# Conditioning vector, input and modulation in one layout: two small loads instead of five

## The chip, the cores and the metric

The kernel runs on one core of a Trainium2 chip. The metric is device time in microseconds (us), the median over several executions. Times inside the profile come from one profiled execution of the kernel and are measured from the start of its span. The engines are TensorE (PE in the profile, its weight loads PEld), VectorE (DVE), ScalarE (ACT), GpSimd (POOL) and SyncE (SP), which issues all loads here.

## The reference

One decode step of a transformer block whose layer norms are modulated by a conditioning vector (adaLN). Two batch elements with one token each, model width 512, 32 query heads of 128 on 8 key/value heads, a cache of 32768 positions of which the last 4096 are used, a feed-forward width of 1792. All data are float32.

```python
mod = (silu(c) @ w_mod).reshape(2, 6, 1, 512)
sa, ca, ga, sb, cb, gb = (mod[:, i] for i in range(6))
h = layernorm(x) * (1 + ca) + sa
q = (h @ wq)                                  # 32 heads of 128
p = softmax(q @ k_cache[:, :, -4096:].T / sqrt(128))
o = p @ v_cache[:, :, -4096:]                 # each of 8 kv heads serves 4 query heads
x = x + ga * (o @ wo)
h = layernorm(x) * (1 + cb) + sb
out = x + gb * (silu(h @ w1) @ w2)
```

The shapes: c and x (2, 512), w_mod (512, 3072), wq (512, 4096), wo (4096, 512), w1 (512, 1792), w2 (1792, 512), and 2 MB of keys and 2 MB of values for each of the 16 pairs of batch element and kv head.

## The kernel before

**The stream.** All large loads go through one ring of eight buffers of 16 KB per partition (`stream`, L69), and all of them are issued on the SyncE queue in the order of the program: four row blocks of w_mod (`wm`), four of wq (`wqt`), then per kv head two loads of keys and two of values (`load_k`, `load_v`), then wo in four loads, w1 in three and w2 in five (`load_runs`, L91). A load waits until the buffer that it takes has been read for the last time by the engine that uses it, eight loads before. `load_rows` (L72) reads 128 successive rows of a weight, one row per partition. `load_runs` gives partition p the rows lo to hi of the group of rows that starts at p times `per`, so that a partition's piece is contiguous in memory and the pieces of neighbouring partitions stand `per` rows apart.

**Two layouts of a vector of 512.** Both put the two batch elements' 512 numbers on eight partitions that lie 16 apart (`rows8`, L104), since VectorE transposes blocks of 32 x 32. In the spread form partition 32g + 16b holds the 128 successive numbers of group g; `turned` (L268) transposes it with a stride of 4 elements, after which partition p holds the numbers 4p to 4p + 3. In the other form, here called the chunk form (names ending in `_ch`), the row holds four runs of 32 numbers that stand 128 apart; a plain transpose (L235 for `cT`, L263 for `hq_T`) then gives partition p the numbers p, 128 + p, 256 + p and 384 + p. The layout of a transposed vector must agree with the rows of the weight that it multiplies: chunk form with 128 successive rows, spread form with rows 4p + k.

**The start.** c and x are loaded in the chunk form, by one load for each batch element (L107), between the first and the second load of w_mod. VectorE transposes c, ScalarE and VectorE form silu (`silu_exp`), and TensorE multiplies with w_mod: shift and scale of the first norm go to `m_ch` (L246) in the chunk form, the other four modulation vectors to `m_sp` (L249) in the spread form. Layer-norm statistics of x come from `moments` (L209). The modulated `h_a` is transposed to `hq_T` and multiplied with wq (L285), and the queries are laid out for the attention. x is read a second time in the spread form (`x_sp`, L474), in the program between the loads of wo and w1, for the residual additions (`xT` at L475, L613).

**The middle.** For each kv head, VectorE transposes the keys (`keys`, L337), TensorE forms scores (L349), then follow the maxima, exponentials, their transposition and the product with the values (L423). `inorder` fixes the order of the instructions of this part on their engines; outside it the framework chooses the order from data dependencies.

**The end.** wo, the second norm, w1, silu and w2 are worked off as their loads land; small matmuls on unused data (`busy`, L534) lie between them. One store of 4 KB (L656) writes the output.

Of the kernel before, what the change touches and what calls it, by code (L numbers as in the profile page):

```python
# [10 lines left out]
ALU = mybir.AluOpType  # L11
AX = mybir.AxisListType

P = 128
B, D = 2, 512
HQ, HKV, DH = 32, 8, 128
# [7 lines left out]
def adaln_block(  # L24
# [16 lines left out]

    nc = tc.nc
    SK = k_cache.shape[2]
    W = min(4096, max(256, SK // 4))
# [14 lines left out]
    def const(shape, name):  # L63
        return consts.tile(shape, F32, name=name)

    def bank(tag, name):
        return (psum1 if tag in "CO" else psum).tile([P, 512], F32, tag=tag, name=name)

    def stream(name):  # L69
        return ring.tile([P, 4096], F32, tag="st", name=name)  # L70

    def load_rows(name, w, k, width):  # L72
        t = stream(f"{name}{k}")[:, :width]
        nc.sync.dma_start(t, w[k * P : (k + 1) * P, :])
        return t

    def load_k(b, h):
        t = stream(f"k{h}_{b}")
        nc.sync.dma_start(
            t, k_cache[b, h, SK - W :, :].rearrange("(p n) d -> p (n d)", p=P)  # L80
        )
        return t
# [8 lines left out]
    def load_runs(name, w, per, lo, hi):  # L91

        e = w.shape[1]
        t = stream(f"{name}{lo}")[:, : (hi - lo) * e].rearrange("p (q e) -> p q e", e=e)
        nc.sync.dma_start(t, w.rearrange("(p q) e -> p q e", q=per)[:, lo:hi, :])
        return t


    x2 = x.rearrange("b s d -> (b s) d")
    x_sp, x_ch, c_ch = const([P, P], "x_sp"), const([P, P], "x_ch"), const([P, P], "c_ch")  # L100
    for t in (c_ch, x_ch, x_sp):
        nc.vector.memset(t, 0.0)
    wm = [load_rows("wm", w_mod, 0, 6 * D)]
    rows8 = lambda t: t.rearrange("(ab r) m -> ab r m", r=16)[:, 0, :]  # L104
    for t, src in ((c_ch, c), (x_ch, x2)):
        for b in range(B):
            nc.sync.dma_start(  # L107
                rows8(t)[b : 2 * 4 : 2, :].rearrange("a (k c) -> a k c", k=4),
                src[b, :].rearrange("(k a c) -> a k c", k=4, a=4),
            )  # L110
# [82 lines left out]

    oTn = const([P, 32, 32], "oTn")
    nc.gpsimd.memset(oTn, 0.0)
    mod_ch = const([P, 2, P], "mod_ch")
# [36 lines left out]

    cT = const([P, 4, 32], "cT")
    nc.vector.transpose(cT.rearrange("p k r -> p (k r)"), c_ch)  # L235
    sg = silu_exp(cT, "sgc", [P, 4, 32])
    scT = const([P, 4, 32], "scT")
    nc.vector.tensor_mul(scT, cT, sg)
    m_ch = bank("A", "m_ch")[:, : 2 * P]
    m_sp = bank("D", "m_sp")  # L240
    for k in range(4):
        ab = wm[k][:, : 2 * D].rearrange("p (s k a c) -> p a s k c", s=2, k=4, a=4)
        cd = wm[k][:, 2 * D :].rearrange("p (s g m) -> p g s m", s=4, g=4)
        for g in range(4):
            r = slice(32 * g, 32 * g + 32)
            nc.tensor.matmul(m_ch[r, :], scT[:, k, :], ab[:, g], start=(k == 0), stop=(k == 3))  # L246
        for g in range(4):
            r = slice(32 * g, 32 * g + 32)
            nc.tensor.matmul(m_sp[r, :], scT[:, k, :], cd[:, g], start=(k == 0), stop=(k == 3))  # L249
        if k == 0:  # L250
            mean_a, rstd_a = moments(x_ch, "a")
            xn = once.tile([P, P], F32, tag="xp", name="xn_a")
            nc.vector.tensor_scalar(
                xn, x_ch, mean_a, rstd_a, op0=ALU.subtract, op1=ALU.mult
            )

    nc.vector.tensor_copy(mod_ch[:, 0, :], m_ch[:, :P])
    nc.vector.tensor_scalar(mod_ch[:, 1, :], m_ch[:, P:], 1.0, None, op0=ALU.add)
    h_a = once.tile([P, P], F32, tag="pr", name="h_a")
    nc.vector.tensor_mul(h_a, xn, mod_ch[:, 1, :])  # L260
    nc.vector.tensor_add(h_a, h_a, mod_ch[:, 0, :])
    hq_T = const([P, 4, 32], "hq_T")
    nc.vector.transpose(hq_T.rearrange("p k r -> p (k r)"), h_a)  # L263
# [4 lines left out]
    def turned(t, name):  # L268
        o = const([P, 4, 32], name)
        nc.vector.transpose(o, t.rearrange("p (m k) -> p k m", k=4))  # L270
        return o


    hT, uT = const([P, 4, 32], "hT_b"), const([P, F // P, 32], "uT")
# [6 lines left out]
    for k in range(4):  # L281
        wv = wqt[k].rearrange("p (n s g m) -> p n g s m", n=2, s=4, g=G)
        for n in range(2):
            for g in range(G):
# [4 lines left out]
                    start=(k == 0),  # L289
                    stop=(k == 3),  # L290
                )
    for n in range(2):
        qT = once.tile([P, D], F32, tag="wide", name=f"qT{n}").rearrange("p (s j r) -> p s j r", s=4, r=32)
        nc.vector.transpose(qT.rearrange("p s j r -> p (s j r)"), q_ps[n])  # L294
        for g in range(G):
            r = slice(32 * g, 32 * g + 32)
# [8 lines left out]
        for i in range(4):  # L305
            r = slice(32 * i, 32 * i + 32)
# [167 lines left out]
    nc.sync.dma_start(rows8(x_sp), x2.rearrange("b (g m) -> g b m", m=P))  # L474
    xT = turned(x_sp, "xT")  # L475
    w1t = []
    for lo, hi in ((0, 2), (2, 3), (3, 4)):
# [17 lines left out]
    for r in (0, 64):  # L495
# [4 lines left out]
            start=True,  # L500
            stop=True,
# [46 lines left out]
    for q in range(24):  # L548
        g = q % 4
# [4 lines left out]
            start=(q < 4),  # L554
            stop=(q >= 20),
# [3 lines left out]
    for q in range(24, 32):  # L559
        for g in range(4):  # L560
# [4 lines left out]
                start=(q == 24),  # L565
                stop=(q == 31),
# [26 lines left out]
    for k in range(4):  # L593
        for g in range(4):
# [4 lines left out]
                start=(k == 0),  # L599
                stop=(k == 3),  # L600
# [16 lines left out]
    for b in range(B):  # L617
# [5 lines left out]
            op0=ALU.mult,  # L623
            op1=ALU.add,
# [4 lines left out]
    for tt in range(WIDE):  # L629
        g = tt % 4  # L630
# [4 lines left out]
            start=(tt < 4),  # L635
            stop=(tt >= WIDE - 4),
# [4 lines left out]
    for tt in range(WIDE, T2):  # L641
        for g in range(4):
# [4 lines left out]
                start=(tt == WIDE),  # L647
                stop=(tt == T2 - 1),
# [35 lines left out]
```

## Time and profile before

| | |
|---|---|
| median of 3 runs | 237.28 us (236.99 to 237.31) |
| the profiled execution, time | 236.89 us |
| the profiled execution, span | 235.0 us |
| busy: PE, DVE, ACT, POOL | 62%, 49%, 11%, 4% of the span |
| data queue of the DMA engines | 7592 packets, 97.54 MB, 97.5% of the time of 16 engines |
| mean granted clock of TensorE | 0.869 |

The span runs from the first to the last instruction; the rest of the execution's time lies around it. A busy share is an average over all stages. The page also cuts the span into 40 slices of 5.9 us with the busy tenths of each engine and the rate of the DMA traffic, and follows the chain of work that ended last from the end to the start.

### The profile page before, as it was taken

The page shows a single profiled execution, that of the slowest core. Times are in us where ns is not written, and L with a number is a line of the kernel's source. Part 1 is how long each engine was busy: PE and PEld are TensorE (multiplying, and loading weights), DVE is VectorE, ACT ScalarE, POOL GpSimd, SP SyncE. Part 2 cuts the span into 40 slices and gives each one's busy share as a digit, 9 for nine tenths or more (in the row PEclk, how much of TensorE's full clock was granted, in tenths as well). Part 3 has the DMA queues.
Part 4 walks back from the last instruction along what each step waited for, and adds up shares of the span by engine and source line. Part 5 has one row for each costly group of instructions (what it writes and reads, how often), then busy time and mean ns, then how long its engine had stood idle before and what let it go on. Part 6 is the DMA issues. An engine that isn't in the chain of part 4 may idle for free.

```text
span 235.0 us, 2644 instructions
## 1 busy us (share of the span) xinstructions
PE 146.5 (62%) x1094; PEld 45.9 (20%) x1094; DVE 114.6 (49%) x176; ACT 25.4 (11%) x56; POOL 10.3 (4%) x30
## 2 busy tenths in 40 slices
PE   0086546367187577667549519626743967788993
PEld 0032101101011121121112102111211222335332
DVE  0634000793694792693892792595298050002130
ACT  2200000100300200200200200200020021003210
POOL 8600000100000000000000000000000000000000
PEclk9999975759869997999976967965985799999999
DMA  6999999999999999999999999999999999999991
GB/s 253 426 438 427 427 438 427 424 439 427 429 441 424 427 438 427 429 438 424 429 435 429 427 432 432 432 429 432 428 429 429 429 432 429 432 426 422 421 412 56
DMA packets 7603, 97.69 MB, mean 416 GB/s; under 512 B 920, under 2 KB 936, under 8 KB 1576
## 3 DMA queue, kind: packets, MB, share of 16 engines
q1 hardware_dynamic: 7592, 97.54, 97.5%
q8 instruction: 8, 0.13, 0.2%
q14 instruction: 3, 0.02, 0.0%
HBM read 97.53 MB, written 0.00 MB: 415 GB/s over the span
## 4 chain that ended last, share of the span: by engine, by line
DMA 64%; DVE 22%; PE 10%; ACT 2%; issue 1%; SPq 1%; DVEq 0%
DVE kT L337 16%; DMA wo<-in_A_wo_dram 14%; DMA k<-in_A_k_cache_dram 14%; DMA v<-in_A_v_cache_dram 13%; DMA wq<-in_A_wq_dram 13%; DMA w<-in_B_w_dram 7%; PE s L349 5%; DMA wm<-in_w_mod_dram 3%; DVE zp L395 2%; PE o L423 2%; PE q L285 1%; DVE xp L393 1%; ACT pr L381 1%; DVE mx L359 1%; ACT L381 1%
## 5 line engine op out<-in xcount | busy, mean ns | idle before, releaser
L337 DVE STREAM_TRANSPOSE kT<-k 128x1024 f32<-128x1024 f32 x64 | 73.7, 1210 | 1.6 <-DMA k<-in_A_k_cache_dram 1.6
L349 PE MATMUL s<-kT,qbd 128*32 128x512 f32 x256 | 44.5, 670 | 11.2 <-DVE kT L337 11.1
L423 PE MATMUL o<-v,ptb 128*32 128x512 f32 x256 | 38.5, 730 | 19.8 <-DMA v<-in_A_v_cache_dram 19.3
L359 DVE TENSOR_REDUCE mx<-s 128x1 f32<-128x512 f32 x8 | 5.5, 691 | 40.1 <-PE s L349 40.1
L349 PEld LDWEIGHTS s<-kT,qbd 128*32 128x32 f32 x256 | 11.1, 126 | 45.8 <-issue 24.1
L285 PE MATMUL q<-wq,hq_T 128*32 128x512 f32 x64 | 11.2, 836 | 10.1 <-DMA wq<-in_A_wq_dram 10.1
L423 PEld LDWEIGHTS o<-v,ptb 128*32 128x32 f32 x256 | 8.1, 124 | 35.8 <-issue 33.1
L402 PE MATMUL pT<-zp,id 128*32 128x256 f32 x64 | 5.6, 418 | 13.9 <-DVE zp L395 13.9
L379 ACT COPY bias<-bp 128x1 f32<-128x1 f32 x8 | 1.3, 159 | 111.9 <-PE bp L377 111.9
L537 PE MATMUL junk<-selh,id 128*32 128x256 f32 x46 | 11.3, 380 | 0.0
L294 DVE STREAM_TRANSPOSE qT<-q 128x512 f32<-128x512 f32 x2 | 1.4, 718 | 18.6 <-PE q L285 18.3
L395 DVE TENSOR_TENSOR zp<-xp,group 128x1024 f32<-128x1024 f32 x8 | 9.8, 1225 | 0.2
L393 DVE STREAM_TRANSPOSE xp<-pr 128x512 f32<-128x512 f32 x8 | 5.6, 701 | 4.4 <-ACT pr L381 4.4
L217 PE MATMUL mean_a<-mv_a,avg 128*128 128x1 f32 x2 | 0.6, 362 | 10.6 <-DVE mv_a L214 10.6
L361 PE MATMUL mT<-ident,mx 128*1 128x128 f32 x16 | 3.0, 270 | 6.4 <-DVE mx L359 6.4
L550 PE MATMUL acc_o<-wo,oTn 128*32 128x512 f32 x48 | 5.8, 598 | 1.9 <-DMA wo<-in_A_wo_dram 1.6
L537 PEld LDWEIGHTS junk<-selh,id 128*32 128x32 f32 x46 | 5.0, 110 | 6.7 <-issue 3.5
L438 PE MATMUL o_all<-ob,selh 128*64 128x128 f32 x64 | 5.7, 304 | 0.8 <-ACT ob L432 0.8
L270 DVE STREAM_TRANSPOSE xT<-x_sp 128x128 f32<-128x128 f32 x1 | 0.4, 403 | 11.8 <-DMA x_sp<-in_A_x_dram 11.8
L432 ACT COPY ob<-o 128x512 f32<-128x512 f32 x8 | 4.7, 585 | 10.3 <-PE o L423 10.3
L285 PEld LDWEIGHTS q<-wq,hq_T 128*32 128x32 f32 x64 | 2.1, 128 | 18.8 <-DMA wq<-in_A_wq_dram 12.5
L249 PE MATMUL m_sp<-wm,scT 128*32 128x512 f32 x32 | 5.7, 796 | 0.0
(132 smaller groups left out, 95.0 us busy)
## 6 DMA issues: line engine op xcount, KB each, us to landing
k<-in_A_k_cache_dram SPq DMA_DIRECT2D x16, 2048.0 KB, 30.2
v<-in_A_v_cache_dram SPq DMA_DIRECT2D x16, 2048.0 KB, 31.5
wq<-in_A_wq_dram SPq DMA_DIRECT2D x4, 2048.0 KB
wo<-in_A_wo_dram SPq DMA_DIRECT2D x4, 2048.0 KB, 32.3
wm<-in_w_mod_dram SPq DMA_DIRECT2D x4, 1536.0 KB, 10.2
w<-in_B_w_dram SPq DMA_DIRECT2D x2, 1024.0 KB, 23.2
w<-in_B_w_dram SPq DMA_DIRECT2D x1, 1792.0 KB
w<-in_B_w_dram SPq DMA_DIRECT2D x2, 896.0 KB
```

The source lines that it names most:

```text
L249: nc.tensor.matmul(m_sp[r, :], scT[:, k, :], cd[:, g], start=(k == 0), stop=(k == 3))
L285: nc.tensor.matmul(q_ps[n][32 * g : 32 * g + 32, :], hq_T[:, k, :], wv[:, n, g], start=(k == 0), stop=(k == 3),)
L337: inorder(nc.vector.transpose(kT[h, b][:, :, 8 * n4 : 8 * n4 + 8, :].rearrange("p j n k -> p n j k"), kt[h, b][:, n4 * 1024 : (n4 + 1) * 1 ...
L349: inorder(nc.tensor.matmul(s_ps[h][r : r + 32, :], qbd[h // 4][:, h % 4, b, j, :], kT[h, b][:, j, 16 * c : 16 * c + 16, :], start=(j == 0) ...
L359: inorder(nc.vector.tensor_reduce(mx, s_ps[h], axis=AX.X, op=ALU.max))
L393: inorder(nc.vector.transpose(xp, pr[h]))
L395: inorder(nc.vector.tensor_mul(zp, xp[:, None, :, 0:16].to_broadcast([P, 4, 16, 16]), group[:, :, None, None].to_broadcast([P, 4, 16, 16]),))
L402: inorder(nc.tensor.matmul(tp[32 * i : 32 * i + 32, :], id4, zp.rearrange("p a s x -> p (a s) x")[:, :, 4 * i : 4 * i + 4], start=True, st ...
L423: inorder(nc.tensor.matmul(o_ps[h][32 * c : 32 * c + 32, :], ptb[h % 2][:, 256 * b + 32 * w : 256 * b + 32 * w + 32], vt[h, b][:, 512 * w ...
L438: inorder(nc.tensor.matmul(o_all[r : r + 64, :], selh[:, m, HQ - G - G * h : 3 * HQ - G - G * h], o_sb[h][:, m * DH : (m + 1) * DH], start ...
L537: inorder(nc.tensor.matmul(junk[0:32, :256], id4, selh.rearrange("p m y -> p (m y)")[:, :256], start=True, stop=True,))
L550: inorder(nc.tensor.matmul(acc[32 * g : 32 * g + 32, :], oTn[:, q, :], wot[q // 8][:, q % 8, :], start=(q < 4), stop=(q >= 20),))
```

## The change

The chunk form goes. c and x are loaded once each, both batch elements by one load, into the spread form (`c_sp`, `x_sp`) at the place where the four small loads stood; the later load of `x_sp` goes too. Row blocks of w_mod and wq are read by `load_runs` with the rows 4p + k for block k, through the helper `row4`; `load_rows` goes. `cT` and `hq_T` are made by `turned`, which moves ahead of its first use. Shift and scale of the first norm come out in the spread form (`m_a`, `mod_a`), so that the matmuls read runs of 128 columns of w_mod instead of 32. The sizes and numbers of the large loads and of the matmuls stay, and one memset on VectorE goes.

```diff
-    def load_rows(name, w, k, width):
-        t = stream(f"{name}{k}")[:, :width]
-        nc.sync.dma_start(t, w[k * P : (k + 1) * P, :])
-        return t
...
-    x_sp, x_ch, c_ch = const([P, P], "x_sp"), const([P, P], "x_ch"), const([P, P], "c_ch")
-    for t in (c_ch, x_ch, x_sp):
+    x_sp, c_sp = const([P, P], "x_sp"), const([P, P], "c_sp")
+    for t in (c_sp, x_sp):
         nc.vector.memset(t, 0.0)
-    wm = [load_rows("wm", w_mod, 0, 6 * D)]
+    row4 = lambda name, w, k: load_runs(name, w, 4, k, k + 1)[:, 0, :]
+    wm = [row4("wm", w_mod, 0)]
     rows8 = lambda t: t.rearrange("(ab r) m -> ab r m", r=16)[:, 0, :]
-    for t, src in ((c_ch, c), (x_ch, x2)):
-        for b in range(B):
-            nc.sync.dma_start(
-                rows8(t)[b : 2 * 4 : 2, :].rearrange("a (k c) -> a k c", k=4),
-                src[b, :].rearrange("(k a c) -> a k c", k=4, a=4),
-            )
-    wm += [load_rows("wm", w_mod, k, 6 * D) for k in range(1, 4)]
-    wqt = [load_rows("wq", wq, k, HQ * DH) for k in range(4)]
+    for t, src in ((c_sp, c), (x_sp, x2)):
+        nc.sync.dma_start(rows8(t), src.rearrange("b (g m) -> g b m", m=P))
+    wm += [row4("wm", w_mod, k) for k in range(1, 4)]
+    wqt = [row4("wq", wq, k) for k in range(4)]
...
-    cT = const([P, 4, 32], "cT")
-    nc.vector.transpose(cT.rearrange("p k r -> p (k r)"), c_ch)
+    def turned(t, name):
+        o = const([P, 4, 32], name)
+        nc.vector.transpose(o, t.rearrange("p (m k) -> p k m", k=4))
+        return o
+
+    cT = turned(c_sp, "cT")
...
-    m_ch = bank("A", "m_ch")[:, : 2 * P]
+    m_a = bank("A", "m_a")[:, : 2 * P]
...
-        ab = wm[k][:, : 2 * D].rearrange("p (s k a c) -> p a s k c", s=2, k=4, a=4)
+        ab = wm[k][:, : 2 * D].rearrange("p (s g m) -> p g s m", s=2, g=4)
...
-            nc.tensor.matmul(m_ch[r, :], scT[:, k, :], ab[:, g], start=(k == 0), stop=(k == 3))
+            nc.tensor.matmul(m_a[r, :], scT[:, k, :], ab[:, g], start=(k == 0), stop=(k == 3))
...
-            mean_a, rstd_a = moments(x_ch, "a")
+            mean_a, rstd_a = moments(x_sp, "a")
...
-    hq_T = const([P, 4, 32], "hq_T")
-    nc.vector.transpose(hq_T.rearrange("p k r -> p (k r)"), h_a)
+    hq_T = turned(h_a, "hq_T")
...
-    nc.sync.dma_start(rows8(x_sp), x2.rearrange("b (g m) -> g b m", m=P))
     xT = turned(x_sp, "xT")
```

More of the change, by code (lines that the diff above doesn't have):

```diff
@@ L195, in adaln_block @@
     nc.gpsimd.memset(oTn, 0.0)
-    mod_ch = const([P, 2, P], "mod_ch")
+    mod_a = const([P, 2, P], "mod_a")
     mod_sp = const([P, 4, P], "mod_sp")
@@ L250, in adaln_block @@
         if k == 0:
-            mean_a, rstd_a = moments(x_ch, "a")
+            mean_a, rstd_a = moments(x_sp, "a")
             xn = once.tile([P, P], F32, tag="xp", name="xn_a")
             nc.vector.tensor_scalar(
-                xn, x_ch, mean_a, rstd_a, op0=ALU.subtract, op1=ALU.mult
+                xn, x_sp, mean_a, rstd_a, op0=ALU.subtract, op1=ALU.mult
             )
-    nc.vector.tensor_copy(mod_ch[:, 0, :], m_ch[:, :P])
-    nc.vector.tensor_scalar(mod_ch[:, 1, :], m_ch[:, P:], 1.0, None, op0=ALU.add)
+    nc.vector.tensor_copy(mod_a[:, 0, :], m_a[:, :P])
+    nc.vector.tensor_scalar(mod_a[:, 1, :], m_a[:, P:], 1.0, None, op0=ALU.add)
     h_a = once.tile([P, P], F32, tag="pr", name="h_a")
-    nc.vector.tensor_mul(h_a, xn, mod_ch[:, 1, :])
-    nc.vector.tensor_add(h_a, h_a, mod_ch[:, 0, :])
-    hq_T = const([P, 4, 32], "hq_T")
-    nc.vector.transpose(hq_T.rearrange("p k r -> p (k r)"), h_a)
+    nc.vector.tensor_mul(h_a, xn, mod_a[:, 1, :])
+    nc.vector.tensor_add(h_a, h_a, mod_a[:, 0, :])
+    hq_T = turned(h_a, "hq_T")
     nc.scalar.copy(mod_sp.rearrange("p s m -> p (s m)"), m_sp)
@@ L266, in adaln_block @@
     ga, sb, cb1, gb = (mod_sp[:, s, :] for s in range(4))
[L268 to L271, printed above, removed]
     hT, uT = const([P, 4, 32], "hT_b"), const([P, F // P, 32], "uT")
```

## The prediction

> **What bounds the kernel now.** I read the page first: the span, the slices and the traffic of the DMA engines, and the chain that ended last.
>
> ```profile
> span 235.0 us, 2644 instructions
> ...
> DMA  6999999999999999999999999999999999999991
> GB/s 253 426 438 427 427 438 427 424 439 427 429 441 424 427 438 427 429 438 424 429 435 429 427 432 432 432 429 432 428 429 429 429 432 429 432 426 422 421 412 56
> DMA packets 7603, 97.69 MB, mean 416 GB/s; under 512 B 920, under 2 KB 936, under 8 KB 1576
> ...
> DMA 64%; DVE 22%; PE 10%; ACT 2%; issue 1%; SPq 1%; DVEq 0%
> ```
>
> The DMA digits stand at 9 from the second slice to the last but one, and the rate there keeps between 412 and 441 GB/s. The chain goes through DMA for 64% of the span. So this is one stream of loads, 97.69 MB of traffic at an almost constant rate, and the kernel ends a fixed stretch after that stream does. The profiled execution took 236.89 us, of which 235.0 us are the span and 1.89 us lie around it; it stands 0.39 us below the median of 237.28 us.
>
> Then I cut the stream into the stages that the change touches (columns: window, its length, busy time of PE, PEld, DVE, ACT and POOL, granted clock, DMA share, GB/s).
>
> ```profile
> 3.00:6.00 3.00, 0.00 (x0) 0.00 (x0) 0.00 (x0) 0.00 (x0) 3.00 (x8) 1.00 1.00 426
> 6.00:7.00 1.00, 0.00 (x0) 0.00 (x0) 0.00 (x0) 0.00 (x0) 1.00 (x3) 1.00 1.12 438
> 7.00:10.00 3.00, 0.00 (x0) 0.00 (x0) 2.91 (x11) 0.00 (x0) 2.44 (x5) 1.00 0.98 410
> 10.00:17.00 7.00, 4.88 (x32) 2.39 (x36) 2.81 (x12) 1.85 (x3) 0.00 (x0) 1.00 1.00 428
> 17.00:40.00 23.00, 12.87 (x96) 2.85 (x92) 2.45 (x9) 0.58 (x1) 0.53 (x1) 0.82 1.01 432
> 40.00:200.00 160.00, 101.25 (x696) 28.46 (x688) 100.93 (x119) 17.47 (x45) 0.94 (x4) 0.83 1.01 431
> 200.00:210.00 10.00, 7.96 (x61) 3.22 (x65) 0.27 (x1) 0.00 (x0) 0.00 (x0) 1.00 1.01 429
> 210.00:215.00 5.00, 4.21 (x62) 2.26 (x58) 0.40 (x1) 1.87 (x2) 0.00 (x0) 1.00 1.00 426
> 215.00:228.00 13.00, 11.84 (x118) 5.00 (x107) 3.75 (x18) 1.77 (x3) 0.00 (x0) 1.00 1.00 419
> ```
>
> 6 to 7 us is where the small loads of c and x pass through, 7 to 17 us holds the rest of w_mod, 17 to 40 us wq as it is read now, 40 to 200 us the k and v loads. In 200 to 210 us wo passes, which L95 reads with 8 successive rows per partition out of 32, thus 16 KB for each partition at a pitch of 64 KB. That is the very pattern that wq gets (4 rows of 16 KB for each partition, one taken). The last row has the loads of w1 and w2, pieces of 14 KB down to 2 KB at a pitch of 28 KB.
>
> Last, the SyncE queue in the timeline (start, duration, what), the piece of the chain by order of time that follows the start, and two of SyncE's waits (total, times, longest).
>
> ```profile
> 0.73 0.40 SPq L74 DMA_DIRECT2D wm<-in_w_mod_dram  x1
> 1.19 1.29 SPq L107 DMA_DIRECT2D c_ch<-in_c_dram  x2
> 2.53 1.09 SPq L107 DMA_DIRECT2D x_ch<-in_A_x_dram  x2
> 3.65 1.40 SPq L74 DMA_DIRECT2D wm<-in_w_mod_dram  x3
> 6.91 1.81 SPq L74 DMA_DIRECT2D wq<-in_A_wq_dram  x4
> 16.14 5.23 SPq L79 DMA_DIRECT2D k<-in_A_k_cache_dram  x4
> ...
> 181.60 0.58 SPq L474 DMA_DIRECT2D x_sp<-in_A_x_dram  x1
> 184.77 31.75 SPq L95 DMA_DIRECT2D w<-in_B_w_dram  x8
> ```
>
> ```profile
> 8.28 30.69 DMA wq<-in_A_wq_dram
> ```
>
> ```profile
> SPq L95 <- PE o L423: 12.7, 4, 6.6
> SPq L79 <- PE m_sp L249: 11.0, 4, 7.3
> ```
>
> The four small issues stand between the first and the second load of w_mod. The stream doesn't notice their issue time: the second w_mod load is issued from 3.65 us on, and the DMA engines are still busy with the first until past 6 us, for cT, which waits for c, starts at 7.09 us and the window 3 to 6 us runs at 426 GB/s. The chain agrees: it leaves the first issue straight into DMA and stays there until wq has landed at 8.28 + 30.69 = 38.97 us.
>
> **The change, part by part.** *The small loads at the start.* Four loads (two of c, two of x, 16 pieces of 128 B each) become two (8 pieces of 512 B each). On SyncE this removes about half of 1.29 + 1.09 = 2.38 us, 1.2 us, so the three later w_mod loads are issued about 1.2 us earlier, at some 2.45 us. They queue behind the first one, so the issue time is worth 0; the cover is the 3 us of work between 3.65 us and the end of the first load, and the 1.2 us would begin to count only if that work were gone. On the DMA engines the removed pieces cost what the stream loses where they pass. In 6 to 7 us it runs at 438, above the 431 of the steady stretch: cost 0. Put on them also the 410 GB/s of 7 to 10 us, and it is 3 x (1 - 410/431) = 0.15 us. The bounds are 0 and -0.15 us, and since two loads stay I take -0.07 us, half the larger end. I see no reason for a loss here.
>
> *The last w_mod, the wq and the first k loads.* The first wq load is issued at 6.91 us, the ninth issue on the queue, when the first w_mod load has landed. With two loads fewer ahead, that hold should fall on the third wq load instead. The queue then still holds three w_mod loads, so nothing runs dry. The first k load is held by a ring slot: it waits for the modulation's matmuls (7.3 us at the longest) and is issued at 16.14 us, while the work in the queue lasts to 38.97 us. This cover of 22.8 us is what hides the whole early chain, c to scT to the modulation to h_a to q.
>
> *That chain's operations.* The transposes of c and h_a now read with a stride of 4 elements, as xT does already.
>
> ```profile
> 7.09 0.31 DVE L235 STREAM_TRANSPOSE cT<-c_ch 128x128 f32<-128x128 f32 x1 [5.75 <-DMA c_ch<-in_c_dram]
> ...
> 21.37 0.31 DVE L263 STREAM_TRANSPOSE hq_T<-h_a 128x128 f32<-128x128 f32 x1
> ...
> 213.28 0.40 DVE L270 STREAM_TRANSPOSE xT<-x_sp 128x128 f32<-128x128 f32 x1 [11.79 <-DMA x_sp<-in_A_x_dram]
> ...
> 216.19 0.32 DVE L572 STREAM_TRANSPOSE aoT<-ao 128x128 f32<-128x128 f32 x1 [2.50 <-PE ao L561]
> ```
>
> From 313 and 311 ns (cT, hq_T) to the 403 ns of xT, both together +0.18 us, against one memset less. The modulation's matmuls for shift and scale keep their count and size, and read runs of 128 elements instead of 32. All of it lies inside the 22.8 us: worth 0. If the cover were gone, 0.2 us would be the price.
>
> *The x_sp load near the end.* One DMA of 0.58 us issue leaves the SyncE queue at 181.60 us, between the wo and the w1 loads. The next issue on the queue came at 184.77 us, 2.6 us after x_sp's was over, because L95 waits for ring slots that the matmuls of L423 free (12.7 us in all); with x_sp gone it still waits. On the engines the 4 KB are at most what 210 to 215 us loses: 5 x (1 - 426/431) = 0.06 us; bounds 0 and -0.06 us, I take the middle, -0.03 us, as the w1 pieces that begin in this stretch would give part of the dip by themselves. VectorE waits 11.8 us for that load, and queued behind the waiting transpose is aoT, which starts at 216.19 us only when TensorE has the attention output, 2.5 us after xT has ended. So the wait hides in idle time, and it is worth 0. What is late next is the same ao as before. At the start, xT waits for a load that the layer-norm statistics need anyway, so VectorE gets no new wait.
>
> *The rows of w_mod and wq.* Every load keeps its 128 pieces, 12 KB for w_mod and 16 KB for wq, but the pieces no longer lie one behind the other: their pitch becomes 48 KB and 64 KB. For wq the price stands in the trace: wo with the same pieces and pitch runs at 429 against 432, so 8.39 MB cost 19.56 instead of 19.42 us, +0.14 us at most; below nothing it can't go, as all these rows share one ceiling. The two rates differ no more than 428 and 432 do for two contiguous loads, so I take 0. For w_mod no load has its pitch; nearest are wo (64 KB pitch, 0 lost) and, at the worst, the 419 GB/s of w1 and w2: 6.29 MB x (1/0.419 - 1/0.428) = +0.32 us. I take 0, by wo, whose pieces are nearest in size.
>
> *The end.* Nothing behind the last landing is touched.
>
> ```profile
> 231.16 0.16 PEld L643 LDWEIGHTS acc_y<-w,uT 128*32 128x32 f32 x8 [0.26 <-DMA w<-in_B_w_dram]
> ```
>
> From the arrival of the last weight at 231.16 us to the end of the span it is 3.84 us, before and after.
>
> The sum: -0.07 - 0.03 = -0.10 us, with terms of 0 for the issues, the chain and the pitch. On the profiled execution that is 236.8 us, on the median 237.28 - 0.10 = 237.2 us. With all gains at their larger ends it is 237.28 - 0.21 = 237.1 us, with all losses 237.28 + 0.14 + 0.32 = 237.7 us.
>
> **The rivals.** *Faster: the small loads are what spoils the ramp.* The stream is thin from 1.5 to 3.0 us, just when the small issues are being worked off.
>
> ```profile
> 1.50:2.00 0.50, 0.00 (x0) 0.00 (x0) 0.00 (x0) 0.50 (x1) 0.50 (x2) 1.00 1.55 270
> 2.00:2.50 0.50, 0.00 (x0) 0.00 (x0) 0.00 (x0) 0.02 (x1) 0.50 (x4) 1.00 0.20 49
> 2.50:3.00 0.50, 0.00 (x0) 0.00 (x0) 0.00 (x0) 0.00 (x0) 0.50 (x3) 1.00 0.63 221
> ```
>
> Against 431 GB/s the second and third of these half microseconds lose 0.5 x (1 - 49/431) + 0.5 x (1 - 221/431) = 0.44 + 0.24 = 0.69 us. If that dip comes from the 64 little pieces of four issues at 1.19 to 3.62 us getting in the way of the first load, two issues with 16 pieces could remove up to three quarters of it, 0.5 us, and with the 0.21 us above the time is 237.28 - 0.7 = 236.6 us. For it: the coincidence in time, and that 270 GB/s in the first half microsecond are 135 KB or 11 pieces of 12 KB, so five of the 16 engines begin later than the others. Against it: a share of 1.55 says that the pieces begun there last longer than the window, so the dip behind them is in the main their own duration, and the small pieces pass only at 6 to 7 us.
>
> *Slower: pieces that lie apart are read more slowly.* The place is w_mod and wq, 14.68 MB or 34.06 us at 431 GB/s. At the 419 GB/s of the stretch with the smallest pieces read at a pitch they take 35.04 us, so the price is 0.98 us and the time 237.28 + 0.98 = 238.3 us. It decides from a rate of 425 GB/s, which costs the 0.47 us that can be measured. The first load, whose places nothing has opened, would feel it most. For it: 48 KB is a pitch that this trace doesn't have, and the w1 and w2 stretch is slower than the rest. Against it: wo at 64 KB runs at 429, and the pieces of w1 and w2 are also smaller.
>
> The Trainium skill (DMA: Bandwidth & Descriptors, section Latency and other measured facts) has such a rule: pieces of 16 KiB for 128 partitions, at a row pitch that is a large power of two, come to 207 GB/s for each direction of a copy at 512 KiB and to 103 at 4 MiB, where a padded pitch gives 214. It has no figure for 64 KB; if the 3% of 512 KiB held there, both tensors would take some 1.1 us more, an estimate from that page, on the side of this rival. The 429 GB/s of wo at 64 KB, 0.5% below 431, don't show it.
>
> *No effect at all: the DMA engine that ends last carries no small piece.* A load of 16 or 8 small pieces need not touch every engine; if one that it doesn't touch ends the stream, even the 0.10 us is not seen. That gives 237.3 us, inside the forecast's range.
>
> **How the numbers follow.** A measurement of this kernel tells about 0.2%, 0.47 us, from no change; the three runs before lie 0.32 us apart. I give the forecast (with the last rival, 237.1 to 237.7 us) 0.70, the faster rival 0.18, and the slower one 0.12. The forecast lies within 0.47 us of 237.28 us. The faster rival's 236.6 us is over the bound, the slower one's 238.3 us too, so these are the chances of faster, same and slower. The range must leave out no more than 0.2: it takes in the forecast's ends, the faster rival as far as 236.6 us, and on the other side half of the slower rival's way, to 237.8 us; what lies beyond is most of the 0.12 and a small part of the 0.18.
>
> **What would show it.** In the changed profile: the stream's rate at 432 in 17 to 40 us and near 428 in 10 to 17 us (pitch free), the second w_mod issue near 2.4 us with the 3 to 6 us window unchanged (issue hidden), cT and hq_T near 0.40 us each, no SyncE issue between wo and w1, and a last landing within 0.3 us of 231.16 us. A rate below 425 in those windows would prove the pitch wrong, and a ramp above 200 GB/s in 2.0 to 2.5 us would prove the faster rival right.

## The result and the profile after

The changed kernel takes 237.66 us (median of 15 runs, 237.23 to 237.98), the kernel before 237.08 us beside it (15 runs, 236.98 to 237.31): 0.58 us more between the medians, 0.24%. The ratio over all runs is 1.0019 with a 95% interval of 1.0012 to 1.0025, which is 0.3 to 0.6 us. So the change stands at the edge of the 0.2% (0.47 us) that the prediction called no change, and is clear of zero all the same, on the other side of zero from the forecast of -0.10 us. The profiled execution took 237.66 us with a span of 235.5 us.

The page after: span, DMA slices, traffic, chain.

```profile
span 235.5 us, 2639 instructions
...
DMA  7999999999999999999999999999999999999991
GB/s 246 408 433 430 431 429 429 437 424 434 431 426 440 423 429 437 434 420 434 434 429 429 431 431 426 440 429 426 437 426 427 434 429 426 440 425 416 427 408 49
DMA packets 7535, 97.69 MB, mean 415 GB/s; under 512 B 844, under 2 KB 868, under 8 KB 1508
...
DMA 53%; DVE 26%; PE 16%; ACT 3%; issue 1%; SPq 0%; DVEq 0%
```

It is still one stream: the DMA digits stand at 9, though the chain now goes through DMA for 53% of the span instead of 64%. The bytes are the same 97.69 MB, and the mean rate falls from 416 to 415 GB/s. The second slice has 408 GB/s where it was 426, but that alone says little, for another slice, the 18th, has 420 where it was 438. The stages are longer and scatter less (columns as before, the last is GB/s).

```profile
3.00:6.00 3.00, 0.00 (x0) 0.00 (x0) 0.00 (x0) 0.00 (x0) 3.00 (x8) 1.00 0.98 393
6.00:7.00 1.00, 0.00 (x0) 0.00 (x0) 0.04 (x1) 0.00 (x0) 1.00 (x3) 1.00 0.97 402
7.00:10.00 3.00, 0.00 (x0) 0.00 (x0) 2.89 (x9) 0.43 (x2) 2.44 (x5) 1.00 1.01 406
10.00:17.00 7.00, 5.28 (x35) 2.39 (x39) 2.88 (x15) 1.43 (x2) 0.00 (x0) 1.00 1.00 425
17.00:40.00 23.00, 12.74 (x92) 2.80 (x88) 2.45 (x9) 0.59 (x1) 0.53 (x1) 0.79 1.01 431
40.00:200.00 160.00, 104.89 (x698) 29.05 (x690) 101.10 (x119) 17.47 (x45) 0.95 (x4) 0.84 1.01 431
200.00:210.00 10.00, 8.77 (x54) 3.03 (x57) 0.27 (x1) 0.00 (x0) 0.00 (x0) 0.83 1.01 429
```

From 17 us on all rows agree with those before within 2 GB/s. Between 3 and 7 us the stream runs at 393 and 402 instead of 426 and 438, so the loss is in by the end of w_mod. To have it in one number, here is the stretch that holds the ramp and all of w_mod, first of the kernel before, then of the changed one.

```profile
0.00:18.00 18.00, 5.88 (x36) 2.58 (x40) 6.22 (x26) 3.14 (x4) 8.83 (x25) 1.00 0.91 371
```

```profile
0.00:18.00 18.00, 6.28 (x48) 2.87 (x52) 6.17 (x26) 3.14 (x4) 8.83 (x25) 1.00 0.91 364
```

371 - 364 = 7 GB/s over 18 us are 126 KB, 0.29 us at 431 GB/s. A mean doesn't show the engine that is latest. The trace has sixteen records of landing for each load, which I read as one for each of the 16 DMA engines. Those of the fourth w_mod load lie on average at 17.73 us before and 18.07 us after, 0.34 us later; the last of them comes at 18.00 us before and 18.63 us after, 0.63 us later. The view of the w_mod loads has the same in its own terms (duration of the issues, start of the first and the last one; then the time from issue to landing, of which the longest is the fourth load's, issued at 4.62 and 3.56 us), first before, then after.

```profile
L74 SPq DMA_DIRECT2D wm<-in_w_mod_dram x4: 396/430/448, 0.7 to 4.6; - x4
DMA to landing us min/median/max: 7.0/10.2/13.4
```

```profile
L88 SPq DMA_DIRECT2D wm<-in_w_mod_dram x4: 389/453/561, 0.7 to 3.6; - x4
DMA to landing us min/median/max: 6.5/10.2/15.1
```

So the whole loss is there when w_mod has landed, and about half of it is that the latest engine has fallen further behind the others. The later landings carry it on: wq had landed at 38.97 us before, and the chain by order of time now says

```profile
7.66 31.89 DMA wq<-in_A_wq_dram
```

so 39.55 us, 0.58 us later. The last weight's arrival moves by as much:

```profile
231.78 0.16 PEld L630 LDWEIGHTS acc_y<-w,uT 128*32 128x32 f32 x8 [0.26 <-DMA w<-in_B_w_dram]
```

231.78 instead of 231.16 us, 0.62 us. What was lost in the first 18 us is carried unchanged to the end; from there to the end of the span it takes 3.72 us (3.84 before), so the tail is 0.12 us shorter.

SyncE and VectorE did what the prediction said. Their rows in the timeline:

```profile
1.19 0.72 SPq L100 DMA_DIRECT2D c_sp<-in_c_dram  x1
1.96 0.57 SPq L100 DMA_DIRECT2D x_sp<-in_A_x_dram  x1
2.57 1.55 SPq L88 DMA_DIRECT2D wm<-in_w_mod_dram  x3
4.16 3.94 SPq L88 DMA_DIRECT2D wq<-in_A_wq_dram  x4
...
184.27 32.86 SPq L88 DMA_DIRECT2D w<-in_B_w_dram  x8
...
6.96 0.41 DVE L226 STREAM_TRANSPOSE cT<-c_sp 128x128 f32<-128x128 f32 x1 [5.76 <-DMA c_sp<-in_c_dram]
...
10.32 0.40 DVE L226 STREAM_TRANSPOSE xT<-x_sp 128x128 f32<-128x128 f32 x1
...
20.57 0.40 DVE L226 STREAM_TRANSPOSE hq_T<-h_a 128x128 f32<-128x128 f32 x1
```

The second w_mod load is issued at 2.57 us instead of 3.65, two of the wq loads follow at once and the others when the first w_mod load has landed. No small load stands between wo and w1 any more. The transposes take 0.41 and 0.40 us, and xT sits in the early idle time.

### The profile page after: what moved, and what is told of

Same layout as the page of the kernel before. It is cut to its first block, busy times and chain, and to the rows that moved or that the text cites. A ratio compares the mean times of both kernels' runs of the same rounds, so it can differ in the third digit from the quotient of the medians.

```text
span 235.5 us, 2639 instructions
## 1 busy us (share of the span) xinstructions
PE 151.8 (64%) x1094; PEld 46.4 (20%) x1094; DVE 114.3 (49%) x175; ACT 25.4 (11%) x56; POOL 10.3 (4%) x30
## 2 busy tenths in 40 slices
DMA packets 7535, 97.69 MB, mean 415 GB/s; under 512 B 844, under 2 KB 868, under 8 KB 1508
## 4 chain that ended last, share of the span: by engine, by line
DMA 53%; DVE 26%; PE 16%; ACT 3%; issue 1%; SPq 0%; DVEq 0%
DVE kT L325 19%; DMA v<-in_A_v_cache_dram 14%; DMA wq<-in_A_wq_dram 14%; DMA wo<-in_A_wo_dram 13%; PE s L337 9%; DMA w<-in_B_w_dram 8%; DMA wm<-in_w_mod_dram 3%; DVE zp L383 3%; ACT pr L369 2%; PE q L273 2%; PE o L411 2%; DVE xp L381 2%; DVE mx L347 1%; PE acc_o L537 1%; PE mT L349 1%
## 5 line engine op out<-in xcount | busy, mean ns | idle before, releaser
L337 PE MATMUL s<-kT,qbd 128*32 128x512 f32 x256 | 47.4, 686 | 10.4 <-DVE kT L325 10.4
L273 PE MATMUL q<-wq,hq_T 128*32 128x512 f32 x64 | 12.8, 942 | 10.3 <-DMA wq<-in_A_wq_dram 10.3
L537 PE MATMUL acc_o<-wo,oTn 128*32 128x512 f32 x48 | 7.4, 744 | 1.2 <-DMA wo<-in_A_wo_dram 0.9
L365 PE MATMUL bp<-negscale,mrow 1*128 1x1 f32 x16 | 3.0, 256 | 4.2 <-DVE mrow L358 4.2
```

The source lines that it names most:

```text
L273: nc.tensor.matmul(q_ps[n][32 * g : 32 * g + 32, :], hq_T[:, k, :], wv[:, n, g], start=(k == 0), stop=(k == 3),)
L337: inorder(nc.tensor.matmul(s_ps[h][r : r + 32, :], qbd[h // 4][:, h % 4, b, j, :], kT[h, b][:, j, 16 * c : 16 * c + 16, :], start=(j == 0) ...
L537: inorder(nc.tensor.matmul(acc[32 * g : 32 * g + 32, :], oTn[:, q, :], wot[q // 8][:, q % 8, :], start=(q < 4), stop=(q >= 20),))
```

## The experiments

Each kernel ran beside the kernel before on one chip; ratios are to that kernel, with 95% intervals, and differences are between medians.

**Which part of the change costs?** Three kernels with one part each, and a fourth, `mix`, with all of it but the rows of w_mod and the single load of c.

`wm_rows`, from the kernel before:

```diff
-    wm = [load_rows("wm", w_mod, 0, 6 * D)]
+    wm = [row4("wm", w_mod, 0)]
...
-    wm += [load_rows("wm", w_mod, k, 6 * D) for k in range(1, 4)]
+    wm += [row4("wm", w_mod, k) for k in range(1, 4)]
```

> The kernel before, with only w_mod read as rows 4p + k; c stays in its old form, so the modulation multiplies rows that don't belong together, and only the time counts. Theory A (the scattered rows of w_mod make the first packets of the stream long, while nothing later changes): about +0.45 us over the kernel before, with the windows 0 to 10 us some 0.15 MB short. Theory B (the two small loads, issued earlier and followed earlier by the large ones, disturb the first loads): 0.0 us. Theory C (the pitch of wq): 0.0 us.

237.50 against 236.92 us, +0.58 us, ratio 1.0026 (1.0016 to 1.0035). The whole loss. In this kernel the stretch from 7 to 10 us is low, where the kernel before has 410 GB/s and the changed one 406:

```profile
7.00:10.00 3.00, 0.00 (x0) 0.00 (x0) 2.87 (x11) 0.00 (x0) 2.44 (x5) 1.00 1.00 381
```

`wq_rows`, from the kernel before:

```diff
-    wqt = [load_rows("wq", wq, k, HQ * DH) for k in range(4)]
+    wqt = [row4("wq", wq, k) for k in range(4)]
```

> The kernel before, with only wq read as rows 4p + k, so the queries are formed from rows that don't belong together, and only the time counts. Theory A: 0.0 us over the kernel before, 17 to 40 us at 431 to 432 GB/s. Theory B: 0.0 us. Theory C: about +0.45 us and a lower rate in 17 to 40 us.

236.91 against 236.92 us, ratio 1.0001 (0.9992 to 1.0009). The pitch of 64 KB is free.

`small_only`, from the changed kernel, where `rows` reads 128 successive rows:

```diff
-    wm = [row4("wm", w_mod, 0)]
+    wm = [rows("wm", w_mod, 0)]
...
-    wqt = [row4("wq", wq, k) for k in range(4)]
+    wqt = [rows("wq", wq, k) for k in range(4)]
```

> The changed kernel with w_mod and wq read as 128 successive rows again, so only the two small loads and the spread form of c, x and the modulation remain of the change; rows and layout don't agree, and only the time counts. Theory A: as the kernel before, -0.1 to 0.0 us, with 3 to 6 us back at 426 GB/s. Theory B: about +0.45 us. Theory C: 0.0 us.

236.94 against 236.92 us, ratio 1.0003 (0.9994 to 1.0012). Two small loads instead of five, issued earlier, bring nothing and cost nothing that can be told.

`mix`, from the changed kernel:

```diff
-    for t, src in ((c_sp, c), (x_sp, x2)):
-        nc.sync.dma_start(rows8(t), src.rearrange("b (g m) -> g b m", m=P))
+    for b in range(B):
+        nc.sync.dma_start(
+            rows8(c_ch)[b : 2 * 4 : 2, :].rearrange("a (k c) -> a k c", k=4),
+            c[b, :].rearrange("(k a c) -> a k c", k=4, a=4),
+        )
+    nc.sync.dma_start(rows8(x_sp), x2.rearrange("b (g m) -> g b m", m=P))
...
-    wm += [row4("wm", w_mod, k) for k in range(1, 4)]
+    wm += [rows("wm", w_mod, k) for k in range(1, 4)]
```

> c in the old form by two loads, so that w_mod can be read as successive rows; x by one load in the spread form, the modulation in the spread form and wq as rows 4p + k, as in the changed kernel. It computes the whole block. Theory A: -0.1 to 0.0 us against the kernel before. Theory B: between 0 and +0.45 us, as three small loads stand there. Theory C: about +0.45 us.

236.94 against 236.92 us, ratio 1.0001 (0.9992 to 1.0009). With w_mod read in successive rows the block takes the time of the kernel before. (The cut leaves out the helper `rows` and the transposition of c in its old form.) The first 18 us of the four, in this order:

```profile
0.00:18.00 18.00, 5.87 (x40) 2.63 (x44) 6.18 (x26) 3.14 (x4) 8.83 (x25) 1.00 0.91 360
```

```profile
0.00:18.00 18.00, 5.87 (x44) 2.71 (x48) 6.02 (x26) 3.14 (x4) 8.83 (x25) 1.00 0.92 370
```

```profile
0.00:18.00 18.00, 6.28 (x40) 2.70 (x44) 6.24 (x26) 3.14 (x4) 8.83 (x25) 1.00 0.91 374
```

```profile
0.00:18.00 18.00, 5.72 (x36) 2.54 (x40) 6.31 (x26) 3.14 (x4) 8.83 (x25) 1.00 0.91 372
```

360 stands alone, the three others are at 370 to 374. Of the three theories A is left, as far as it names the place: w_mod's rows, in the beginning of the stream.

**The first load, the pattern, or the size of the pieces?** Four more. `wm0_rows` is the kernel before with only the first line of `wm_rows` changed.

> The kernel before, with only the first of the four w_mod loads read as rows 4p; rows and layout don't agree there, only the time counts. Theory A1 (the scattered rows hurt because nothing has yet read this memory: the first load opens all of it): most of the loss, +0.3 to +0.6 us over the kernel before. Theory A2 (a piece of 12 KB at a pitch of 48 KB is read more slowly wherever it stands, so each load carries a quarter): +0.15 us, hardly to be told from 0.

237.02 against 237.06 us, ratio 0.9998 (0.9990 to 1.0007). The first load alone at the pitch costs nothing, although it is the first to read across all of w_mod: theory A1 falls in this form. Yet its rate from 3 to 6 us is lower still than that of the changed kernel:

```profile
3.00:6.00 3.00, 0.00 (x0) 0.00 (x0) 0.00 (x0) 0.00 (x0) 3.00 (x8) 1.00 0.93 373
```

373 GB/s here with no time lost: the low 393 GB/s of this stretch in the changed kernel doesn't by itself stand for its loss either.

`v_plain` and `v_rows` replace four value loads of the kernel before:

```diff
-                vt[h - 1, b] = load_v(b, h - 1)
+                if h - 1 in (2, 3):
+                    k = 2 * (h - 3) + b
+                    t = stream(f"v{h - 1}_{b}")
+                    nc.sync.dma_start(t[:, : 6 * D], w_mod[k * P : (k + 1) * P, :])
+                    vt[h - 1, b] = t
...
# v_rows instead:
+                    nc.sync.dma_start(t[:, : 6 * D], w_mod.rearrange("(p q) e -> p q e", q=4)[:, k, :])
```

> The kernel before, with four of the value loads (heads 2 and 3) replaced by a second read of w_mod in 128 successive rows of 12 KB each, as the base for the next kernel; the output isn't the block's, only the time counts. Both theories: 2.1 MB less in the stream, so about -4.9 us.

> As the kernel with the four value loads replaced, but with the rows 4p + k of w_mod in them, so the pattern of the changed w_mod loads stands in the middle of the stream; only the time counts. Theory A1: the same as with successive rows, 0.0 us, and no long packets there. Theory A2: +0.5 us over it, with a lower rate in the stretch where these four loads pass.

232.27 and 232.26 us, ratios 0.9798 (0.9785 to 0.9811) and 0.9797 (0.9784 to 0.9811). The stretch where these loads pass, first with successive rows, then at the pitch:

```profile
92.00:122.00 30.00, 19.93 (x144) 6.16 (x147) 24.17 (x26) 3.79 (x10) 0.00 (x0) 0.89 1.01 430
```

```profile
92.00:122.00 30.00, 21.95 (x158) 5.93 (x150) 21.19 (x24) 3.79 (x10) 0.00 (x0) 0.98 1.00 428
```

430 and 428 GB/s for 30 us, and the same time: the pattern of the changed w_mod loads costs nothing in the middle of the stream. Theory A2 falls too. (w_mod had been read once by then. Every piece of these loads took 460 ns, with either order.)

`wm16`, from the changed kernel:

```diff
-    wm = [row4("wm", w_mod, 0)]
+    wflat = w_mod.rearrange("(p q) e -> p (q e)", q=4)
+    def wm_part(j):
+        t = stream(f"wm{j}")
+        nc.sync.dma_start(t, wflat[:, 4096 * j : 4096 * (j + 1)])
+        return t
+    wm = [wm_part(0)]
...
-    wm += [row4("wm", w_mod, k) for k in range(1, 4)]
+    wm += [wm_part(j) for j in (1, 2)]
```

> The changed kernel, with the four rows of each partition read in three loads of 16 KB pieces instead of four of 12 KB, at the same pitch of 48 KB; the matmuls take their columns from where they land, four more of them for the row that lies in two loads. It computes the whole block. Theory A1: as the changed kernel, +0.4 to +0.6 us over the kernel before. Theory A2: if the pitch is what costs, as the changed kernel; if the size of 12 KB is, as the kernel before.

237.03 against 237.06 us, ratio 0.9998 (0.9989 to 1.0008), and 372 GB/s over the first 18 us:

```profile
0.00:18.00 18.00, 6.48 (x45) 2.87 (x46) 6.27 (x26) 3.14 (x4) 8.96 (x25) 1.00 0.91 372
```

So at the same pitch and place, w_mod in pieces of 16 KB is free. Together with the middle of the stream this says that the loss needs the beginning and the way in which the changed kernel cuts w_mod there. `wm16` changes three things at once, the size of the pieces, the places where they begin (all at multiples of 16 KB) and the number of loads, three instead of four; which of them matters is not shown.

**Which loads, and what of the beginning?** `wm13_rows` and `wm02_rows` are the kernel before with two of the four loads through `row4`, k = 1 and 3, or k = 0 and 2.

> The kernel before, with only the second and the fourth w_mod load read at the pitch of 48 KB (rows 4p + 1 and 4p + 3); rows and layout don't agree there, only the time counts. The packets of these two loads were the long ones in the profiles with all four loads at the pitch. Theory R (the loss belongs to these two row sets, whose pieces begin at odd multiples of 12 KB): +0.5 us over the kernel before. Theory S (any load at the pitch behind the first one pays in the start of the kernel): about two thirds, +0.35 us.

> The kernel before, with only the first and the third w_mod load read at the pitch of 48 KB (rows 4p and 4p + 2); only the time counts. Theory R: 0.0 us over the kernel before. Theory S: +0.15 to +0.2 us, from the third load.

On one chip 237.31 and 236.99 us against 237.13 us; ratios 1.0008 (0.9999 to 1.0017) and 0.9994 (0.9986 to 1.0003). Against the kernel before each is inconclusive. Against each other they differ by 0.32 us, and their runs don't overlap (237.16 to 237.37, 236.88 to 237.12). So the odd rows cost more than the even ones, but less than the 0.5 us of theory R. And the two, +0.18 and -0.14 us, don't add up to the 0.58 us of all four loads: the loads at the pitch cost more together than apart, and why is not shown.

`pad_plain` puts two loads that nothing uses ahead in the kernel before; `pad_rows` has w_mod through `row4` behind them.

```diff
+    for i in range(2):
+        pad = ktp.tile([P, 4, 32, 32], F32, tag="kT", name=f"pad{i}")
+        nc.sync.dma_start(
+            pad.rearrange("p a b c -> p (a b c)"),
+            v_cache[i, 0, :W, :].rearrange("(p n) d -> p (n d)", p=P),
+        )
     wm = [load_rows("wm", w_mod, 0, 6 * D)]
```

> The kernel before, with two loads of 2 MB that nothing uses put ahead of the first w_mod load, as the base for the next kernel. All theories: 4.2 MB more in the stream, so about +9.7 us.

> The same two unused loads ahead, and w_mod at the pitch of 48 KB behind them; rows and layout don't agree, only the time counts. Theory S (the pitch costs only while the engines fill their constants, in the first 10 us): the same as with successive rows behind the two loads, 0.0 us. Theory R, or any cost of w_mod's pattern ahead of its first use: +0.5 us over it.

246.84 and 246.71 us, ratios 1.0412 (1.0397 to 1.0426) and 1.0408 (1.0394 to 1.0422). The stretch of w_mod in the two, 11 to 28 us:

```profile
11.00:28.00 17.00, 7.38 (x52) 2.91 (x52) 3.26 (x12) 1.85 (x3) 0.00 (x0) 1.00 1.00 427
```

```profile
11.00:28.00 17.00, 8.12 (x55) 3.12 (x56) 3.26 (x12) 1.85 (x3) 0.00 (x0) 1.00 1.01 429
```

Behind 10 us of other loads the pitch costs nothing, although w_mod hasn't been read before: so neither unread memory nor the pattern as such. Is it then what the other engines do in the first 10 us?

`quiet_plain` and `quiet_rows` move GpSimd's filling of constants, all but the identity, behind the modulation (the cut shows two of the constants):

```diff
-    for t in qg + qbd:
-        nc.gpsimd.memset(t, 0.0)
...
+    def fill(t, flat, value):
+        n = t.shape[0]
+        nc.gpsimd.tensor_copy(flat[:, :1], mod_sp[:n, 2, :1])
+        nc.gpsimd.memset(t, value)
+    for t in qg + qbd:
+        fill(t, t.rearrange("p s b j g -> p (s b j g)"), 0.0)
```

> The kernel before, with GpSimd's filling of constants (all but the identity) held until the modulation is ready, so that the first 20 us of the stream pass without it, as the base for the next kernel. Theories S1 and S2: -0.1 to 0.1 us against the kernel before.

> The same, with w_mod at the pitch of 48 KB; rows and layout don't agree, only the time counts. Theory S1: the same as with successive rows and no long packets in 6 to 10 us. Theory S2: +0.5 us over it.

237.31 and 237.64 us against 237.03 us; ratios 1.0009 (1.0000 to 1.0018) and 1.0025 (1.0016 to 1.0035). The runs don't overlap (237.23 to 237.38, 237.39 to 237.89). The first 18 us:

```profile
0.00:18.00 18.00, 7.46 (x52) 2.95 (x52) 4.77 (x25) 3.14 (x4) 0.70 (x6) 1.00 0.90 371
```

```profile
0.00:18.00 18.00, 7.50 (x52) 2.94 (x52) 4.76 (x25) 3.14 (x4) 0.70 (x6) 1.00 0.91 364
```

GpSimd's filling is out of this stretch, and the pitch costs 0.33 us still, with 364 GB/s against 371: theory S1 falls for GpSimd. (The held filling itself seems to cost some 0.3 us, at the edge of its interval; the cause of that is open. Together the two cost 0.61 us, about as much as the pitch alone in `wm_rows`. What VectorE does in the first microseconds was not moved here.)

`late_plain` and `late_rows` instead hold the large loads until that filling is done (the buffers of wq in the same way):

```diff
+    for k in range(4):
+        wmk = stream(f"wm{k}")[:, : 6 * D]
+        nc.gpsimd.tensor_copy(wmk[:, :1], oTn[:, 0, :1])
+        wm.append(wmk)
+    for k in range(4):
+        nc.sync.dma_start(wm[k], w_mod[k * P : (k + 1) * P, :])
```

> The kernel before, with all large loads held until GpSimd has filled its last constant (it copies one column of zeros into each w_mod and wq buffer then), as the base for the next kernel; the small loads of c and x go ahead alone. All theories: some 9 us over the kernel before.

> The same, with w_mod at the pitch of 48 KB; rows and layout don't agree, only the time counts. Theory S1 (the pitch costs while GpSimd and VectorE fill constants beside it): the same as with successive rows, 0.0 us. Theory S2 (it costs in the first 17 us of the stream itself, wherever that begins): +0.5 us over it.

246.09 and 246.34 us, ratios 1.0381 (1.0367 to 1.0395) and 1.0393 (1.0378 to 1.0407). The intervals overlap; the runs lie at 245.90 to 246.30 and 246.30 to 246.48 us, four and five of them. The stream begins 9 us later, and a loss of some 0.25 us seems to come with it. The two profiled executions, at 246.30 and 246.34 us, can't show it. This speaks weakly for S2, at half the size that it gave.

**Two ways to arrange the changed kernel.** `order0213` loads and multiplies w_mod's row sets in the order 0, 2, 1, 3; `interleave` issues the loads of w_mod and wq in turns.

```diff
# order0213
+    for k in (2, 1, 3):
+        wm[k] = row4("wm", w_mod, k)
...
-    for k in range(4):
+    for k in (0, 2, 1, 3):
# interleave
+    wqt = [row4("wq", wq, 0)]
+    for k in range(1, 4):
+        wm.append(row4("wm", w_mod, k))
+        wqt.append(row4("wq", wq, k))
```

> The changed kernel, with the w_mod loads and their matmuls in the order of rows 4p, 4p + 2, 4p + 1, 4p + 3. It computes the whole block. The long packets stood in the second and the fourth load, which are also the ones with odd rows. If the rows decide, the second load (7 to 10 us) is back at 420 GB/s and above, and the loss moves to the third (10 to 14 us) and the fourth load; if the place in the stream decides, the second stays near 380 to 406 GB/s, and the time is that of the changed kernel, +0.5 us over the kernel before.

> The changed kernel, with the loads of w_mod and wq taking turns, so that three of the four w_mod loads come 5 to 15 us later. It computes the whole block. Theory S2 (the pitch of w_mod costs only in the beginning of the stream): 0.0 to +0.2 us over the kernel before, as only the second w_mod load still passes within the first 17 us. If w_mod's pitch costs ahead of its first use wherever it stands: +0.5 us.

237.23 and 237.29 us against 237.16 us; ratios 1.0000 (0.9991 to 1.0009) and 1.0007 (0.9998 to 1.0015). Their windows of 0 to 18 us:

```profile
0.00:18.00 18.00, 6.28 (x44) 2.77 (x48) 5.99 (x26) 3.14 (x4) 8.83 (x25) 1.00 0.92 367
```

```profile
0.00:18.00 18.00, 6.21 (x36) 2.19 (x36) 6.04 (x26) 3.14 (x4) 8.83 (x25) 1.00 0.92 370
```

With the even rows second, the second load runs freely,

```profile
7.00:10.00 3.00, 0.00 (x0) 0.00 (x0) 2.75 (x9) 0.43 (x2) 2.44 (x5) 1.00 1.03 426
```

as it would if the rows decide (the kernel before has 410 GB/s here); but the loss doesn't move to the third and fourth load, it mostly goes. So neither the rows nor the place decides alone: odd rows as third and fourth load cost next to nothing. By their ratios, each to the kernel before beside it, the first arrangement is just faster than the changed kernel (1.0019, 1.0012 to 1.0025), the second can't be told from it, and neither beats the kernel before.

## Why the prediction was right or wrong

**The stream and its ends: right.** What was lost by the time w_mod had landed, 0.63 us, arrived at the end, 0.58 us at wq and 0.62 us at the last weight, and the tail behind it kept its length to 0.12 us.

**Issue times, the hold on wq, the early chain, x_sp: right.** The second w_mod load was issued at 2.57 us (some 2.45 forecast), the hold fell on the third wq load, cT and hq_T took 0.41 and 0.40 us, and the issue between wo and w1 is gone. `small_only` puts all of it together at a ratio of 1.0003, so the two small terms can't be told from 0; their -0.10 us would also lie within its interval of 0.9994 to 1.0012. The time of the rival in which the engine that ends last carries no small piece fits, but no run shows which engine carries them. Two of the signs failed: the window from 3 to 6 us went from 426 to 393 GB/s, and the last landing moved by more than 0.3 us. The first had been named as a sign for the issue times, and `small_only`, with the same early issues, has lost no time.

**The pitch of wq: right,** by wo's row. `wq_rows` measured 1.0001.

**The pitch of w_mod: wrong; this is the step that failed.** I set it at 0 by wo and bounded it by +0.32 us from the w1 and w2 stretch; alone it measures +0.58 us (`wm_rows`), more than the bound, and with w_mod back in successive rows (`mix`) the ratio is 1.0001. Both rows come from 200 us and later. The trace of before had no row of a load at a pitch in its first 18 us, and I took a row from the steady stream for the beginning. I had even written that the first load would feel it most, and priced a whole ramp for the faster rival, without asking whether the beginning as a whole behaves differently. Nor was it the first load: `wm0_rows` is at 0.9998.

**The slower rival: right in its sign and in naming w_mod, wrong in its mechanism.** A rate lower by a constant for pieces that lie apart (0.98 us) is refuted by `wq_rows`, `v_rows` and `pad_rows`. Its test, a rate below 425 GB/s in 10 to 17 or 17 to 40 us, would have missed the loss: these windows show 425 and 431, and most of the lost bytes are lost before 10 us. The Trainium skill's rule (DMA: Bandwidth & Descriptors, section Latency and other measured facts) on large power-of-two row pitches, stated there from 512 KiB up, doesn't explain this: the pitch of 64 KB, a power of two, is free in `wq_rows`, and the loss comes at 48 KB, which is none and is itself free in `pad_rows` and `wm16`. A pitch of 512 KiB stands in no run here.

**The range: luck.** 236.6 to 237.8 us holds 237.66 us, and so just does the forecast's upper end of 237.7 us. But that end counts +0.14 us for wq, which measured 0, and the kernel before, timed beside the changed one, took 237.08 us instead of the 237.28 us from which the range was worked out. From 237.28 us the same 0.58 us would have led to 237.86 us, past the range.

**What is shown and what stays open.** Shown: the loss is w_mod's row order (`wm_rows`, `mix`); it needs the beginning of the stream (`v_rows`, `pad_rows`); it doesn't need GpSimd's filling beside it (`quiet_rows`), and it is neither unread memory nor the pitch alone; the odd row sets carry it more than the even ones (`wm13_rows`, `wm02_rows`), but not as third and fourth load (`order0213`).

The landings agree. The last w_mod load has landed at 18.63 us in the changed kernel and at 18.65 us in `wm_rows`, but between 17.88 and 18.26 us in `small_only`, `mix`, `wq_rows`, `wm0_rows`, `wm02_rows`, `wm16` and `order0213`, and at 18.41 us in `wm13_rows`. With the held filling it is 18.54 us at the pitch and 18.25 us without (`quiet_rows`, `quiet_plain`).

The trace's records of single packets agree in direction. A piece of 12 KB takes 460 ns in the steady stream. Summed over the 128 pieces of a load, the second w_mod load spends 1.6 us more than that before, 2.9 us in the changed kernel and 5.6 us in `wm_rows`, the fourth 0, 0.8 and 1.7 us, the third next to nothing in all three. Spread over 16 engines, the second and the fourth load together come to 0.1, 0.2 and 0.5 us for each. The first load spends 9.4, 13.2 and 9.8 us more, but also 12.8 us in `wq_rows`, which lost nothing, so its long pieces don't go with the time. Behind the two unused loads no piece is late, with either order.

Open: why a stream in its first 18 us is sensitive to the odd row sets of w_mod in pieces of 12 KB, and why the four loads lose more together than the two pairs. No run here changes the place of the pieces alone, or how far the engines stand apart.

## What to carry to other kernels

A cost read from the steady part of a stream need not bound the same operation in its first microseconds: the beginning has to be priced from rows of the beginning, and where there are none the range must say so. When a layout change lets both sides of a product choose their row order, compare the orders for the first loads of the stream by themselves. Here successive rows (`mix`), larger pieces (`wm16`) and the changed rows in another order (`order0213`) each gave the time of the kernel before, and the scattered order was free where the stream was already running. Look at the engine that lands last, not only at the mean rate: a mean that is lower by 7 GB/s stood for half of the loss. A saving in small loads was worth nothing here that could be told (`small_only`), as their pieces pass behind a transfer that is under way.

## What the runs showed of the hardware

The slow beginning was known from the trace before, but not that what is lost there depends on the order of the rows: the same four loads take 0.58 us more as the first loads (`wm_rows`), and nothing more after 10 us of other traffic (`pad_rows` 246.71 us, `pad_plain` 246.84 us). What the 16 engines have lost against each other by then isn't made up: the last landing of the load before the last one is 0.62 us later than in the kernel before (231.10 against 230.48 us), as after w_mod (0.63 us). And the beginning hardly cares for the small loads, as the half microseconds of the changed kernel show:

```profile
2.00:2.50 0.50, 0.00 (x0) 0.00 (x0) 0.00 (x0) 0.01 (x1) 0.50 (x4) 1.00 0.23 74
2.50:3.00 0.50, 0.00 (x0) 0.00 (x0) 0.00 (x0) 0.00 (x0) 0.50 (x3) 1.00 0.65 246
```

It has 74 and 246 GB/s in the thin part where it was 49 and 221, with 16 small pieces issued instead of 64. Each difference is 25 GB/s for half a microsecond, one piece of 12 KB; both make 0.06 us, not the 0.5 us of the faster rival. `wm_rows`, which keeps all the small loads, has 106 GB/s over the first 3 us, the changed kernel 102 and the kernel before 90, so even this much can't be put down to them.
